# Block products for gate and value of three groups, one ScalarE silu, and a chained out-projection, in an attention and SwiGLU kernel

## The chip, the cores and the metric

The kernel runs on one core of a Trainium2 chip. A core has TensorE (PE in the views, with its weight loads as PEld), which multiplies matrices into the accumulation memory PSUM; VectorE (DVE); ScalarE (ACT); GpSimd (POOL), which does not touch PSUM here; and SyncE (SP), whose queue issues most transfers. The metric is the device time of one execution in microseconds, the median of several runs.

## What is computed

```python
# q, k, v: 4 x 8 heads x 768 x 64; heads 0, 2, 6 see all earlier keys,
# the others only the first 4 keys and a window of 64
scores = scale * q @ k.T;  scores[~mask] = -1e9
a = exp(scores - max) / sum
x = (a @ v).transpose(0, 2, 1, 3).reshape(3072, 512)
g = x @ w_gate                      # 512 x 1536
out = (g * sigmoid(g) * (x @ w_val)) @ w_out     # 1536 x 512
```

## The kernel before

The 3072 tokens are 24 tiles of 128, made in pairs from attention: load q, k and v, cast to 16 bit, transpose (on PE for the early pairs, by DMA for the later ones), scores (L570), exp on ACT (L582), a mask where needed (L590, DVE or POOL), values (L600), division by the sum (L607, L608), and a transpose that gives x with features on the partitions. Four tiles make a group, so there are groups 0 to 5; x of two groups is held at a time (`xt`).

The feed-forward part of a group has 12 tiles of 128 hidden features. A plain gate or value tile is four matmuls of 512 columns (`gate`, L762). The gate goes through tanh on ACT (L768, `g * sigmoid(g)` is `0.5 g (1 + tanh(g/2))`), then DVE multiplies twice: `stt1` (L775) makes `(1 + tanh) * g`, `stt2` (L781) multiplies by half the value and writes the hidden state `h_sb` in 16 bit. Groups 0 to 3 have plain gates and values. Groups 4 and 5 have plain gates, but their values are made of seven block products (Winograd's form of Strassen's scheme): x is cut in two halves of tokens and two of features, the weights in two halves of features and two of hidden features, and seven products of sums of blocks take the place of eight. Sums of weights (`msum`, L1058) and of x (`xsum`, L1088) are made once; `w_product` (L1108) makes one product for a pair s of hidden tiles, four matmuls of 256 columns. Products 1, 6, 7 and 4 are added one upon the other in one PSUM bank X, and after each of the first three a copy of the bank's state (r1, u2, u3) is taken, since the four result blocks need different partial sums. Product 2 goes to a bank Y, products 5 and 3 to a bank Z. The copies and adds (`w_copy`, `w_add` L1129) bring the results to SBUF, and `stt2_w` (L1152) multiplies them with the gate.

The out-projection of every group is made by seven products too (`seventh`, L866; 12 matmuls of 256 columns each), on sums of h (`hsum`, L837) and of w_out (`wsum`, L415). Before the change each product of groups 0 to 4 has a PSUM bank of its own, and DVE adds them up in the output buffer (`gathered`, L904): one copy and seven adds a group. Group 5 has a form of its own (`last_sevens`) that stores each quarter as it comes. Two halves of a group's output are stored each by one transfer.

The order is written out. Every piece of work is a task of a `Plan` with a list of engines that may run it, dependences and the buffers that it takes. `ORDER` lists all tasks, two characters a task, in one line for all engines, made by a planner outside the kernel; each engine runs its own tasks in that order. `WAYS` has a digit a task, which of its engines it takes; `SLOTS` a digit a buffer, which place of its ring. Waits follow from the dependences; every engine's queue is in order, so an instruction that waits holds up all that stand behind it on that engine.

Rings of buffers: `raw` (11 of 4 KB a partition), `hq`, `e`, `sig`, `sil` (casts, exps, tanh, first multiplies), `xb`, `xt`; and eight PSUM banks that `gv` (gate, value, block products), `o` (out-projection) and `big` (scores, attention values: two banks) share.

Of the kernel before, what the change touches and what calls it, by code (L numbers as in the profile page):

```python
# [7 lines left out]
FP = mybir.dt.float32  # L8
FH = mybir.dt.float16
# [7 lines left out]
    "06000307090A01081U1V0D041cxl1W1X0C021d1f0B20211g1e280g1i2229231h2B2A1j0m1r2C0h1Y1p1s2D1a0F1Z2N1q"  # L17
    "2X1b2E0G2O051k1l2W1t1m2F1u2L1x1v1w2f2M1n2g1y2cxk2h0n27252d241o262l2i2e2m2G0E0y2H1z2I2P0z2j2Q8m2t"
    "2R0k8w8n102o308x8o2x112p2U312J0i132V8p2K8z2y0H8q918y2k9G928r3C2n94939L2z8s3I9H323D0q9B95968t149I"
    "8u3J903L978v389C0l99983K9D9E0j2Z9M9A9J3M9F2Y9O9N0o3N9K3U339P1C3V3R2a2q2r0I3S2b9p2s16343O2u3W9k9q"  # L20
    "0r3T3P9r35363b9l2v0J3E379V3X3F1D3H3f3i3Q9Q9m3g0s1F9n9R9W3A3h9S9u0p399o9s9v3B9X2w0K9z179t3j0x3Y9w"
    "3Z0M193u9Y3a3G3l9Z3n3c3m9a1G0uA09T3v9bA13o3d0t409U3k2SA23e9c0O43A33p441A3q41459x3r2T0v42490L9y4C"
    "463y4D9f4H4A3w3x9i9g4B479d9h0P9j3s124Q4K3t4N4R9eB74O1HB24LA6BA48B8B5A7B30QB9184EAd4M0w5C1Q4ZBM15"
    "4F4PBBBP4g4G1BAsA8B40RAYAtB60N4YAxAu1KBNAvA94e5D1IBC1RBO1TAeAgAyAf1J5GATAwBD0SB0Az1EBQ5KAUBH4VAh"
    "4I1MBFBE4h5fA4BG1SAZ0T5EAa5IAi1L5FB1AbBI1OAV4J4aAnAc4bBJAC0VA5AB4fAoAA4d4l4o1NAD5gBK1P3zAG4p5nAE"
    "BL4m4S0aAH4TAjAI5JAp4WAk4U4i5L4q4jAM4v4c4n0W4rAJ5H514y4XANAK4zAF5l4k52AWAL4sAO4tAlAS4u4w0U5T54AX"
    "5m5UAq535055APAr6LAm5W565MAQ57BTBRARBU5o5NBV58BW5c594x5XBf5ABS5O5B5v5p5s5Y5w5VBh5q0YBX5t0XBY5Z5r"
    "5a0ZBd5i5b606366Be64BZ6H676w5P6I6N5QCj6K5uCUBaCk6P6EClCPBcCVBg0bCKCQCW745dCm5R7OCLCF73Cn5hBi69CN"
    "5SCMCR5x5yCOC06O615zCXC16J5e6vC2C3685kBq0f6x6572BjBrCYCGC46Q6ACIBl7P5jCHBt71Bs8e6U6RBk6VCe0eBu0c"
    "CA6WCf626SCg6B6CCJChCB6TCCBvCiCSBw6DBb70C5Bx6G6eCTByC66yBpC77F6X6Z0d7GBzC86YCZ7HC96a757CCa6n6FCb"  # L30
    "Bm6o817Q6b6c76CqCDCs826dDf7DBnCc77BoDr7E89CEE1Ds7WDt7879E2DcCdDu7XCrDdE3CtE4De7UDD7A6MCo6gDvDE7L"
    "7RDgDmDF7BCuE5DGDnCp7VDXCvDHDoDI88DYDZ6z7Y6k7bDJ7S6lDKDS7ZDa6m7j7IDb7JDTDp8f7K7cE6Dq6fDU6p7m6hE7"
    "E8E96i7dDN80EA6jDL6q86Dw7M7a7N6r6sDxDOD06t7nDy6u7p7eD1Cw7x7fDM7q8387DP8A7T8D7sCx8ED2Cz7gD3DV8B7o"
    "DhDW7h7rD47i7t7kDiEaD68NDj85D5Cy8G8YD87u8ZD7DQEc8H7vDR8I8W7y7wEtDk8J8C8X8F8T8QDl8K8L8g8UDzEb8hEu"
    "Ee8O7l8RFNE0EfEv7z848i8jD98MDC8VEg8kF0EhDAElEi8SDBEmFl8lEj8PF1EwF8Fm8aEEExFnEG8bEk8cFpEdF98dEpFq"
    "EnEBF2FrEoFAEyEqF4FBEDEzErF3FCEsECFRFsFFFSF5GcFGEFFtFDFTEHFOEJFoFPFZGYEKFUF6FaEIFEF7FVFbGjFQGZFW"
    "ENFcGdGaFuFXFJFvGeGbFYFdFKGfFxFHFeEOFLFwFyGnFfGkEMGrFIGgGsG1FzGlGhHPG2FMGiG0FhG3GtFgFiEPGoHQGuGm"
    "HLELEQGvHRGpH6GqG5FjERFkHSH7HjG6G4ESH8HkH2G7GwETHlHMG8GxEVGyH3HTGzHNH0EWHUEUEZHOHrHVGCH1HmHvH9HW"
    "HsHnGBEXHtHXHoHwHpHDGEH4HqHYHbEYHxHEGDHHH5HcHAHfHuHBHyHFHCHZG9HIHgHdHGGHGFHhHJHaHzGGHKGLGKI0HeGA"
    "GRGIGJI1HiI3I2I9GNI4GMI5GPI6IBGOGUGSIAGQI7GVGTGWINICI8GXIEIDIRIFIHISITIJIGIIILIKIOIUIMIQIXIVIPIa"  # L40
    "IWIYIZIbIc"
)
WAYS = (
    "000000000000000000000000000000000000000000000000000000000000222222202202202021110101101110110120"
    "212101100000000000000000210012022201011011000000000000002100222212001010000000000001001000000000"
    "001200002221000000001001000000001000010010000000000212210100000000010000002000000100000120010010"
    "000000000100000001200000000000000000000000000000000000000000220000001000000000100000210001001000"
    "002101120020000001001000000021000100100000000021020000000000000000010001202200200000001000000002"
    "100000000000012001020000000000000000000200000000000000001100010000000000000000000000000000000000"
    "000000000000000000000000000000000000000000000000000010000010000000000000000000000000000000000000"  # L50
    "000000000000000000000000000000000000000000000001100000000000000000000000000000000000000000000000"
    "000000000000000000000000000100011100100000000000001000000000000000000000000000000000000000000000"
    "000000000000000001001110001000000000001110110000000001000000000000010000000100000000100000000000"
    "000000000000000000000000000000000000000000011110000110000000000010111100000100001000000000000000"
    "000000000000000000000000000000000000000000000000000000000000000000000111000110000000011001011001"
    "000"
)
# [65 lines left out]
def kernel(  # L123
# [48 lines left out]
    RINGS = {"raw": 11, "hq": 5, "e": 6, "xb": 3, "xt": 2, "sig": 2, "sil": 3,  # L172
             "ps": 8, "gv": 8, "o": 8, "big": 8}
# [7 lines left out]
    for r in ("raw", "hq", "e", "xb", "xt", "sig", "sil"):  # L181
        pools[r] = ctx.enter_context(tc.tile_pool(name="p_" + r, bufs=1))
# [249 lines left out]
    def cast(n, kd, x):  # L432

        if (n, kd) not in hqs:
            hqs[n, kd] = buf("hq", [128, 1024], FH, "hq").rearrange(
                "p (k a x) -> p k a x", k=2, a=4)
# [135 lines left out]
    def exps(t, u, unit):  # L572
        e = es[t, u] = buf("e", [128, 8, 128], FH, "e")
# [63 lines left out]
    def tasks_of_pair(n):  # L637
# [21 lines left out]
        for kd in "qk":  # L659
            old = oldq if kd == "q" else older  # L660
            if n >= XPE:
# [3 lines left out]
                P.uses(cs[kd][0], "hq", *T_ev[n, kd])  # L665
# [10 lines left out]
            P.uses(cs[kd][0], "hq", tr)  # L676

    def tasks_of_tile(t):
# [13 lines left out]
        for u, unit in enumerate(units):  # L692
# [651 lines left out]
```

## Time and profile before

| | |
|---|---|
| runs | 236.73, 236.61, 236.62 us; median 236.62 |
| profiled execution | span 234.7 us from the first to the last instruction; its time as a whole is not on the page |
| instructions | 5854 |

The profile comes from one execution of the program. The span begins with the first instruction. Busy time is that of the engines' own instructions; issuing transfers is not counted. An instruction's row names the output and input tiles (`banks` is PSUM, `raw` a buffer of the raw ring) and the number of partitions by elements. "Idle before" is the time in which the engine did nothing just before the instructions of a group, with what ended it. The chain of waits goes back from the last instruction, at each step to what released it.

The first scores run at 10 us, the first feed-forward product at 19.6; the last exp runs at about 163 us, the last block product at 214, and from 218.3 on PE has only out-projection left, 120 matmuls.

### The profile page before, as it was taken

The numbers are of one execution on the slowest core, as the hardware profiler recorded it, in microseconds if no ns is written. First come the engines' busy times: TensorE is split into PE (matmuls) and PEld (weight loads), VectorE is DVE, ScalarE is ACT, GpSimd is POOL, SyncE is SP. The second block draws the span as 40 slices with busy tenths as digits, with TensorE's granted clock in tenths as the row PEclk, the third lists the DMA queues.
The fourth block names the chain that finished last, engine by engine and source line by source line (L and its number), as shares of the span: only waits on it lengthen the run. The fifth ranks groups of instructions, "written<-read, shape, count | busy, mean of one in ns | idle before, by whom it ended". The sixth has DMA issues, their size and how long they took to land.

```text
span 234.7 us, 5854 instructions
## 1 busy us (share of the span) xinstructions
PE 228.7 (97%) x2283; PEld 152.8 (65%) x2283; DVE 204.4 (87%) x369; ACT 157.9 (67%) x256; POOL 136.4 (58%) x150
## 2 busy tenths in 40 slices
PE   7899999999999999999999999999999999999994
PEld 2577865654457778645564556776876767668883
DVE  1889989989989998989879974889979999999954
ACT  3599999679899779856786389768554643553110
POOL 7485499864695300469840887273096930593950
PEclk9999999999999999999999999999999999999999
DMA  6999999999999998998994621500920000220054
GB/s 180 351 343 366 327 340 369 343 341 314 271 259 220 236 251 166 270 179 178 234 217 124 102 45 31 62 3 2 225 45 3 3 0 3 89 89 4 0 201 159
DMA packets 67196, 40.76 MB, mean 174 GB/s; under 512 B 25184, under 2 KB 61024, under 8 KB 67168
## 3 DMA queue, kind: packets, MB, share of 16 engines
q1 hardware_dynamic: 65104, 37.37, 64.5%
q10 hardware_dynamic: 2064, 3.02, 3.6%
q8 instruction: 18, 0.29, 0.5%
q14 instruction: 10, 0.08, 0.1%
HBM read 28.31 MB, written 6.29 MB: 147 GB/s over the span
## 4 chain that ended last, share of the span: by engine, by line
PE 89%; ACT 3%; DMA 2%; DVE 2%; SPq 2%; issue 1%; POOL 0%; ACTq 0%; POOLq 0%
PE banks L762 45%; PE banks L866 23%; PE banks L1108 8%; PE banks L570 6%; PE banks L600 6%; DMA raw<-in_k_dram 2%; ACT e L582 2%; SPq L352 1%; PE banks L476 1%; PE banks L624 1%; DVE xb L608 1%; ACT kT L209 0%; SPq L357 0%; DVE kT L211 0%; DVE sil L775 0%
## 5 line engine op out<-in xcount | busy, mean ns | idle before, releaser
L762 PE MATMUL banks<-xt,wg_sb 128*128 128x512 f16 (+1 forms) x304 | 71.6, 368 | 0.1
L582 ACT ACTIVATE e<-banks 128x1024 f16<-128x1024 f32 (+2 forms) x68 | 59.4, 911 | 11.0 <-PE banks L570 6.3
L768 ACT ACTIVATE sig<-banks 128x512 f32<-128x512 f32 (+1 forms) x76 | 42.8, 577 | 30.6 <-PE banks L762 23.2
L762 PE MATMUL banks<-xt,wv_sb 128*128 128x512 f16 (+1 forms) x208 | 48.2, 363 | 0.0
L762 PEld LDWEIGHTS <-wg_sb 128*128 128x128 f16 x304 | 28.6, 98 | 25.9 <-issue 0.5
L866 PEld LDWEIGHTS <-h_sb 128*128 128x128 f16 x420 | 40.2, 98 | 7.4
L775 DVE SCALAR_TENSOR_TENSOR sil<-sig,banks 128x512 f32<-128x512 f32 (+1 forms) x52 | 32.8, 641 | 5.8 <-ACT sig L768 4.7
L781 DVE SCALAR_TENSOR_TENSOR h_sb<-sil,banks 128x512 f16<-128x512 f32 (+1 forms) x52 | 32.8, 640 | 3.1 <-PE banks L762 2.7
L837 POOL TENSOR_TENSOR h_sb<-h_sb 128x768 f16<-128x768 f16 x13 | 21.3, 1644 | 21.1 <-DVE hs_sb L837 17.2
L762 PEld LDWEIGHTS <-wv_sb 128*128 128x128 f16 x208 | 19.1, 98 | 17.2
L590 POOL TENSOR_TENSOR e<-e,m 128x640 f16<-128x640 f16 (+1 forms) x16 | 26.6, 1670 | 5.7 <-ACT e L582 4.7
L904 DVE TENSOR_TENSOR out_sb<-banks,out_sb 128x512 f32<-128x512 f32 x37 | 25.0, 684 | 2.1 <-PE banks L866 1.7
L866 PE MATMUL banks<-wt_sb,h_sb 128*128 128x256 f16 x216 | 26.0, 273 | 0.1
L866 PE MATMUL banks<-wo_sb,h_sb 128*128 128x256 f16 x204 | 24.9, 273 | 0.0
L209 ACT COPY raw<-banks 128x512 f32<-128x512 f32 x26 | 14.6, 588 | 15.2 <-DVE h_sb L1152 5.5
L570 PEld LDWEIGHTS <-kT 64*128 64x128 f16 x472 | 14.5, 94 | 9.2 <-issue 8.7
L570 PE MATMUL banks<-qT,kT 64*128 64x128 f16 x472 | 19.9, 218 | 0.1
L211 POOL CAST hq<-raw 128x1024 f16<-128x1024 f32 (+1 forms) x9 | 8.0, 893 | 20.1 <-DMA raw<-in_k_dram 18.2
L600 PEld LDWEIGHTS <-e 128*128 128x128 f16 x472 | 17.3, 97 | 3.6 <-POOL e L590 0.3
L600 PE MATMUL banks<-vt,e 128*128 128x65 f16 x472 | 18.6, 193 | 0.0
L608 DVE TENSOR_TENSOR xb<-banks,rc 128x512 f16<-128x512 f32 x24 | 16.6, 691 | 0.8
L775 DVE SCALAR_TENSOR_TENSOR banks<-sig,banks 128x512 f32<-128x512 f32 x24 | 16.3, 687 | 0.2 <-ACT sig L768 0.2
(85 smaller groups left out, 318.6 us busy)
## 6 DMA issues: line engine op xcount, KB each, us to landing
raw<-in_v_dram SPq DMA_DIRECT2D x12, 512.0 KB, 6.8
raw<-in_q_dram SPq DMA_DIRECT2D x8, 512.0 KB, 5.6
raw<-in_k_dram SPq DMA_DIRECT2D x8, 512.0 KB, 5.0
raw<-in_moe_w_gate_dram SPq DMA_DIRECT2D x6, 512.0 KB, 8.2
raw<-in_moe_w_val_dram SPq DMA_DIRECT2D x6, 512.0 KB, 8.3
raw<-in_moe_w_out_dram SPq DMA_DIRECT2D x6, 512.0 KB, 8.4
out_dram<-out_sb SPq DMA_DIRECT2D x6, 512.0 KB, 3.5
raw<-in_q_dram SPq DMA_DIRECT2D x8, 256.0 KB, 6.6
```

The costliest lines, as they stand in the source:

```text
L570: nc.tensor.matmul(sc[:, c:c + n, :], weights, moving, start=first, stop=last)
L582: nc.scalar.activation(out=to, in_=src, func=AF.Exp, scale=scale)
L590: ENG[task().way].tensor_tensor(out=ev, in0=ev, in1=mm, op=ALU.mult)
L600: nc.tensor.matmul(avs[t][:, odd, n * 66:n * 66 + 65], ee, vv, start=(m == 0), stop=(m == len(bl) - 1))
L608: nc.vector.tensor_tensor(out=xb.rearrange("p n o d -> p o n d"), in0=av[:, :, :, 0:64], in1=rc.to_broadcast([128, 2, 4, 64]), op=ALU.mult)
L762: nc.tensor.matmul(ps, wsb[:, kk, j * 128:(j + 1) * 128], xt[:, kk, c[0]:c[1]], start=(kk == 0), stop=(kk == 3))
L768: nc.scalar.activation(out=sg[g, j, c], in_=gs[g, j, c], func=AF.Tanh, scale=0.5)
L775: nc.vector.scalar_tensor_tensor(out=sl[g, j, c], in0=sg.pop((g, j, c)), scalar=1.0, op0=ALU.add, in1=gs.pop((g, j, c)), op1=ALU.mult)
L781: nc.vector.scalar_tensor_tensor(out=hs[g, j][:, c[0]:c[1]], in0=sl.pop((g, j, c)), scalar=0.5, op0=ALU.mult, in1=vs.pop((g, j, c)), op1=A ...
L837: ENG[T_hs[g, x][part].way].tensor_tensor(out=to, in0=a, in1=b, op=op)
L866: nc.tensor.matmul(rooms[g, p][:, x, lo:hi], left[:, j, 128 * x:128 * x + 128], right[:, j, lo:hi], start=(on is None and (j == 0 if apart ...
L904: nc.vector.tensor_tensor(out=cell(*to), in0=room, in1=plus, op=ALU.add)
```

## The change

- Groups 3, 4 and 5 (`FULL`) have both gate and value made of block products; before, only the values of groups 4 and 5 were. The gate's weight sums lie in the rooms of kT[0] and vt[0] once batch 2 no longer needs them.
- For each pair s of hidden tiles, quarter by quarter (c11, c21, c22, c12: half of tokens by half of hidden features), ACT makes silu in one operation (`AF.Silu`), and DVE one multiply by the value, of which c21 is read straight from bank X and the others from PSUM after an add in place. Groups 0 to 2 keep tanh and two multiplies.
- c11 is one DVE add of bank Y and r1 (before: a copy of Y and an add on POOL or DVE).
- Out-projection of groups 0 to 4: products 1, 6, 7, 4 are chained in one bank, with copies r1, u2, u3 and c21 on ACT or DVE; product 3 is added onto product 5; three DVE adds a group in place of seven. Its sums wait for quarters of h.
- The rings hq, e, sig and sil become one ring `t2` of 16 buffers of 2 KB.
- ORDER, WAYS and SLOTS are new for the whole kernel.

```diff
-    RINGS = {"raw": 11, "hq": 5, "e": 6, "xb": 3, "xt": 2, "sig": 2, "sil": 3,
-             "ps": 8, "gv": 8, "o": 8, "big": 8}
+    RINGS = {"raw": 11, "t2": 16, "xb": 3, "xt": 2, "gv": 8, "o": 8, "big": 8}
...
-    ONTO = {2: 1, 3: 5}
+    ONTO = {True: {2: 1, 3: 5}, False: {6: 1, 7: 1, 4: 1, 3: 5}}
...
-        on = ONTO.get(p) if g == NG - 1 else None
+        on = ONTO[g == NG - 1].get(p)
...
+    def o_copy(g, name):
+        room = rooms[g, {"r1": 1, "u2": 6, "u3": 7, "c21": 4}[name]]
+        if name == "c21":
+            to = cell(1, 0)
+        else:
+            to = o_cells[g, name] = buf("t2", [128, 2, HM], FP, "oc")
+        copy(T_ga[g, name], to, room)
+
+    def o_add(g, name):
+        p, to, other = {"c11": (2, (0, 0), "r1"), "c22": (5, (1, 1), "u3"),
+                        "c12": (3, (0, 1), "u2")}[name]
+        nc.vector.tensor_tensor(out=cell(*to), in0=rooms[g, p], in1=o_cells.pop((g, other)),
+                                op=ALU.add)
...
+        p1 = product(1, quarter[0, 0] + wo, ["o"])
+        r1 = copied("r1", [p1])
...
+        p6 = product(6, T_hs[g, 2] + T_ws[2] + [r1])
+        u2 = copied("u2", [p6])
+        p7 = product(7, T_hs[g, 3] + T_ws[3] + [u2])
+        u3 = copied("u3", [p7])
+        p4 = product(4, quarter[1, 1] + T_ws[4] + [u3])
+        c21 = copied("c21", [p4] + free[1])
...
-    WINO = {"v": (4, 5), "g": ()}
+    FULL = (3, 4, 5)
...
+    SPENT = [kT[0].rearrange("p a b c d -> p (a b c d)"), vt[0].rearrange("p a b c -> p (a b c)")]
...
     def w_add(mat, g, s, name):
-        to = w_cell(mat, g, s, name)
-        other = w_cell(mat, g, s, "y2") if name == "c11" else w_rooms[mat, g, s, "Z"]
-        ENG[T_wc[mat, g, s, name].way].tensor_tensor(out=to, in0=other, in1=to, op=ALU.add)
...
+        on, other = {"c11": ("Y", "r1"), "c22": ("Z", "u3"), "c12": ("Z", "u2")}[name]
+        room, other = w_rooms[mat, g, s, on], w_cells.pop((mat, g, s, other))
+        to = w_cells[mat, g, s, name] = (
+            other if mat == "g" else
+            buf("gv", [128, 2, 256], FP, "gv") if name == "c22" else room)
+        nc.vector.tensor_tensor(out=to, in0=room, in1=other, op=ALU.add)
+
+    def silu(g, s, name):
+        src = w_rooms["g", g, s, "X"] if name == "c21" else w_cells["g", g, s, name]
+        nc.scalar.activation(out=w_cells["g", g, s, name], in_=src, func=AF.Silu)
+
+    def mul(g, s, name):
+        x, y = {"c11": (0, 0), "c21": (1, 0), "c12": (0, 1), "c22": (1, 1)}[name]
+        j = NK * y + 2 * s
+        val = w_rooms["v", g, s, "X"] if name == "c21" else w_cells.pop(("v", g, s, name))
+        nc.vector.tensor_tensor(
+            out=h_sb[:, g % 2, j:j + 2, 256 * x:256 * x + 256], in0=val,
+            in1=w_cells.pop(("g", g, s, name)), op=ALU.mult)
```

What the strings say, counted task by task from ORDER and WAYS (before, after):

| tasks | before | after |
|---|---|---|
| PE: gate tiles / value tiles (of 512 columns; the eight halves of group 0 count as four) | 72 / 48 | 36 / 36 |
| PE: block products of gate and value | 42 | 126 |
| PE: out-projection products | 42 | 42 |
| ACT: tanh of groups 3 to 5 / silu | 36 / 0 | 0 / 36 |
| ACT: copies of block products / of the out-projection | 25 / 6 | 46 / 18 |
| DVE: multiplies of groups 3 to 5 | 72 | 36 |
| DVE: adds / copies of block products | 13 / 5 | 54 / 8 |
| DVE: adds and copies of the out-projection | 43 | 26 |
| POOL: adds of block products / weight sums of gate and value | 5 / 3 | 0 / 9 |
| whole casts of q and k on ACT / DVE / POOL | 10 / 4 / 6 | 6 / 1 / 13 |
| output halves stored from SP / from ACT | 6 / 4 | 8 / 2 |

In the new ORDER PE works from group 2's first out-projection product on as follows (`out2.p1` is product 1 of group 2, `sc20.1` the second set of scores of tile 20, `val` attention values, `wp3.1.6g` product 6 of group 3's gate, pair 1):

```
out2.p1 sc20.0 sc20.1 val19.1 val19.0 out2.p2 sc21.0 sc21.1 sc20.2 out2.p6 val17.1 sc21.2 val17.0
out2.p7 sc22.1 sc22.2 sc22.0 out2.p5 val20.1 val20.0 out2.p4 sc23.3 sc23.2 val21.1 val21.0 out2.p3
wp3.1.1g sc23.1 sc22.3 sc23.0 wp3.2.1g wp3.0.1g wp3.2.2g wp3.1.6g wp3.1.2g wp3.1.2v wp3.0.6g val22.1
val22.0 wp3.1.5g wp3.1.7g wp3.0.7g wp3.0.5g wp3.1.1v wp3.2.6g
```

and ACT around its last exp:

```
ex23.2 oc2.c21 ex22.3 ex23.1 wy3.0.r1g ex23.0 wy3.1.u2g wy3.0.u2g silu3.2.c11 wy3.0.u3g wy3.1.r1v
wy3.2.u2g wy3.0.r1v silu3.1.c21 silu3.1.c11 wy3.2.u3g wy3.1.u2v silu3.0.c21
```

All 68 exps and 40 tanh of the new order stand before its first silu. In the old order the gates and values of group 3 stand among the scores of tiles 16 to 23; in the new one group 3 begins with `wp3.1.1g`, and the last scores (tile 23) stand there too.

More of the change, by code (lines that the diff above doesn't have):

```diff
@@ L22 @@
[L22 to L26, printed above, removed]
@@ L896, in gathered @@
             nc.vector.tensor_tensor(out=c, in0=room[:, x, lo:hi], in1=c, op=ALU.add)
-        elif g == NG - 1 and name == "c11":
+        elif name == "c11":
             x, lo, hi = PARTS[part]
             copy(T_ga[g, name, part], cell(*to)[:, x, lo:hi], room[:, x, lo:hi])
-        elif other is None:
-            copy(T_ga[g, name], cell(*to), room)
         else:
-            plus = ends["r1"] if g == NG - 1 and name == "r6" else cell(*other)
+            plus = ends["r1"] if name == "r6" else cell(*other)
             nc.vector.tensor_tensor(out=cell(*to), in0=room, in1=plus, op=ALU.add)
@@ L1001, in tasks_of_sevens @@
         if g == NG - 1:
-            last_sevens(g, lower, upper, wo, free, old, T_h, product, sums, gather, finish)
+            last_sevens(g, quarter, wo, free, of_part, product, sums, gather, finish)
             return
-        p1 = product(1, lower + wo, ["o"])
-        r1 = gather("r1", [p1] + free[1])
-        sums(1, lambda part: [y for j in range(3 * part, 3 * part + 3)
-                              for y in T_h[j] + T_h[j + NK]] + old)
-        sums(3, lambda part: [T_hs[g, 1][part]])
@@ L1069 @@
                     (lambda mat=mat, i=i, kk=kk: msum(mat, i, kk)),
-                    deps=[y for n in range(6) for y in T_w[mat, n]] + before,
-                    takes=(["hq"] if i == 4 else ["e"]) if mat != EARLY
-                    else [] if kk else ["raw"],
+                    deps=[y for n in range(6) for y in T_w[mat, n]] + before + spent,
+                    takes=["raw"] if mat == "v" and kk == 0 else [],
                     after=T_mw[mat, i][:1]))
@@ new lines @@
+                a = P.add(f"gate{g}.{j}.{c[0]}", ["PE"],
+                          (lambda g=g, j=j, c=c: gate(g, j, c, wg_sb, gs)),
+                          deps=xs[c[0] // 128:c[1] // 128] + [T_w["g", j // 2][j % 2]],
+                          takes=["gv"])
+                th = P.add(f"tanh{g}.{j}.{c[0]}", ["ACT"],
+                           (lambda g=g, j=j, c=c: tanh(g, j, c)), deps=[a], takes=["t2"])
+                s1 = P.add(f"stt1 {g}.{j}.{c[0]}", ["DVE"],
+                           (lambda g=g, j=j, c=c: stt1(g, j, c)), deps=[th], takes=["t2"])
@@ L1253 @@
+                P.uses(a, "gv", s1)
+                P.uses(T_first_x[g], "xt", a)
                 was = [T_p[g - 2, p] for p in ((6, 7) if j < NK else (3, 4))] if g > 1 else []
                 was += T_hs[g - 2, 4] if g > 1 and j < NK else []
-                if g not in WINO["g"]:
-                    P.uses(th, "sig", s1)
-                if g in WINO["v"]:
-                    cells = [T_wc["v", g, j % NK // 2, y] for y in below]
-                    s2 = P.add(f"stt2 {g}.{j}.{c[0]}", ["DVE"],
-                               (lambda g=g, j=j: stt2_w(g, j)), deps=[s1] + cells + was)
-                    T_h.setdefault(j, []).append(s2)
-                    P.uses(*((th, "gv") if g in WINO["g"] else (a, "gv")), s2)
-                    P.uses(T_wc["v", g, j % NK // 2, head], "raw", s2)
-                    continue
+                P.uses(th, "t2", s1)
```

396 lines of the change are left out of this document (168 added, 228 removed).

## The prediction, made before the changed kernel was run

> **What bounds the kernel now.** First the page: the span, the busy shares, the granted clock, and the chain of waits.
>
> ```profile
> span 234.7 us, 5854 instructions
> PE 228.7 (97%) x2283; PEld 152.8 (65%) x2283; DVE 204.4 (87%) x369; ACT 157.9 (67%) x256; POOL 136.4 (58%) x150
> PEclk9999999999999999999999999999999999999999
> PE 89%; ACT 3%; DMA 2%; DVE 2%; SPq 2%; issue 1%; POOL 0%; ACTq 0%; POOLq 0%
> ```
>
> TensorE (PE) is busy 97% of 234.7 us at full clock and carries 89% of the chain that ended last. VectorE (DVE) follows with 87%. Second the view by windows: each row gives the busy microseconds of PE, weight loads, DVE, ScalarE (ACT) and GpSimd (POOL), then clock, DMA share and GB/s. I cut at the stages of the work.
>
> ```profile
> 19.60:67.20 47.60, 47.59 (x486) 29.07 (x486) 44.59 (x88) 42.76 (x69) 34.34 (x39) 1.00 1.13 330
> 67.20:106.50 39.30, 39.29 (x450) 27.14 (x448) 36.08 (x64) 31.81 (x52) 15.39 (x17) 1.00 1.11 222
> 106.50:131.30 24.80, 24.80 (x220) 13.73 (x220) 21.80 (x37) 16.62 (x27) 14.18 (x12) 1.00 0.82 178
> 131.30:158.70 27.40, 27.31 (x311) 17.84 (x309) 20.80 (x37) 20.67 (x32) 19.02 (x22) 1.00 0.32 45
> 158.70:171.00 12.30, 12.30 (x149) 9.14 (x149) 12.02 (x25) 8.16 (x14) 2.87 (x3) 1.00 0.52 119
> 171.00:218.30 47.30, 47.30 (x350) 33.98 (x348) 45.55 (x75) 23.48 (x43) 28.97 (x22) 1.00 0.08 27
> 218.30:234.70 16.40, 13.10 (x120) 11.49 (x118) 10.57 (x19) 1.56 (x3) 7.80 (x5) 0.98 0.36 129
> ```
>
> The reader is to see that from 19.6 to 218.3 us PE is idle for 0.11 us in all, although DVE is at 94% (44.59 of 47.60) in the first stretch and at 96% (45.55 of 47.30) in the last. So end time is PE work, and work of other engines is paid only where it makes PE wait. Third the chain in order of time (start, us, what), for the price of a product:
>
> ```profile
> 57.75 9.50 PE banks L762 x44
> 159.15 0.54 PE banks L1108 x4
> 186.57 1.75 PE banks L1108 x16
> 218.30 13.11 PE banks L866 x120
> 231.43 0.42 DVE out_sb L896
> ```
>
> A 512-column matmul costs 9.50/44 = 0.216 us, a 256-column one 1.75/16 = 0.1094 (13.11/120 gives the same in the out-projection). A gate or value tile is four of the first, 0.864; a block product four of the second, 0.4375.
>
> **TensorE's share of the change.** Gone: 36 gate tiles of groups 3 to 5 and 12 value tiles of group 3, 48 x 0.864 = 41.5 us. Added: 3 groups x 3 pairs of tiles x 2 matrices x 7 = 126 block products where 42 stood, so 84 x 0.4375 = 36.8 us. The balance is **-4.7 us**. The out-projection keeps its 12 matmuls a product. Since PE is never idle before, there is no old wait to win back. Below that I allow 1.4 us more, from fewer changes between short attention matmuls and wide ones (the change row above: 0.54 where 0.4375 is due, so 0.1 a change; 40 changes after the start against 44 give 0.4) and from a start that may shift by 1 us, since some early evacuations change engine.
>
> **The other engines.** Rows of groups (count | busy us, mean ns | idle before), and two of the timeline for the spacing of instructions back to back:
>
> ```profile
> L768 ACT ACTIVATE sig<-banks 128x512 f32<-128x512 f32 x68 | 40.0, 599 | 30.6 <-PE banks L762 23.2 <-DVE banks L775 2.9 <-DVE xb L608 2.8
> L209 ACT COPY raw<-banks 128x512 f32<-128x512 f32 x26 | 14.6, 588 | 15.2 <-DVE h_sb L1152 5.5 <-DVE out_sb L904 4.6 <-PE banks L1108 3.8
> L209 ACT CAST hq<-raw 128x1024 f16<-128x1024 f32 x10 | 10.4, 1043 | 0.1
> L211 POOL CAST hq<-raw 128x1024 f16<-128x1024 f32 x6 | 6.2, 1035 | 18.2 <-DMA raw<-in_k_dram 17.6 <-DVE m L289 0.3 <-POOL vt L211 0.2
> L1152 DVE SCALAR_TENSOR_TENSOR h_sb<-banks,raw 128x512 f16<-128x512 f32 x24 | 15.9, 682 | 0.2
> L1129 POOL TENSOR_TENSOR raw<-raw 128x512 f32<-128x512 f32 x5 | 6.8, 1365 | 12.3 <-ACT raw L209 12.3
> L1058 POOL TENSOR_TENSOR raw<-wv_sb 128x768 f16<-128x768 f16 x3 | 4.9, 1644 | 0.1
> L582 ACT ACTIVATE e<-banks 128x1024 f16<-128x1024 f32 x44 | 44.0, 1025 | 5.0 <-PE banks L570 2.4 <-PE banks L600 1.0 <-issue 0.9
> 196.19 1.89 DVE L1152 SCALAR_TENSOR_TENSOR h_sb<-banks,raw 128x512 f16<-128x512 f32 x3
> 173.10 1.56 ACT L209 COPY raw<-banks 128x512 f32<-128x512 f32 x3 [0.77 <-DVE raw L1129]
> ```
>
> Full-size DVE instructions come every (1.89 - 0.68)/2 = 0.60 us, ACT copies every (1.56 - 0.59)/2 = 0.49. From the strings (counts in the section on the change): DVE loses 72 gate and value multiplies, 13 cell adds, 5 copies and 43 gathers of the out-projection, and gets 36 products, 54 adds, 8 copies and 26 gathers: 133 become 124, -9 x 0.60 = -5.4 us. ACT changes 36 tanh for 36 silu (I take the tanh's 0.60 us; a silu that reads SBUF is not in the trace, and the nearest cast from SBUF, 64x512, took 0.615) and gets 33 more copies, 33 x 0.49 = 16 us; it gives four whole q/k casts away (-4.2). So ACT goes from 158 to about 171, 74% of 232. POOL takes seven of those casts (+7.2) and six weight sums (+9.8) and loses five adds (-6.8), among smaller moves: about 140 of 232. No engine but PE is full on average. These terms I cost at nothing: PE's 232 us cover them. If that cover goes, it goes in one of two places, which are the rivals below. The four extra sums of x for group 3 and the eight of the gate weights lie on POOL and DVE ahead of their products; the weight sums go to rooms of batch 2's keys and values, which the order frees some 13 us of PE work before product 7 first reads them.
>
> Stores: eight halves of the output are issued on SP instead of six. A store waits in SP's queue for its cells, and behind it wait loads and transposes. The one of group 0 stands ahead of the loads of q9, k10, k11, x11 and q10; its cells are due with PE's own order there, so nothing is late. DMA's share is 0.82 and 0.32 in the windows from 106.5 to 158.7, so the last pair's transposes, which move about 18 us of PE work forward, find room.
>
> **The one new instruction outside the sums: a table load.**
>
> ```profile
> L209 ACT ACT_TABLE_LOAD x1 | 1.3, 1283 | 0.7 <-PEq L1325 0.7
> ```
>
> Exp, Tanh and Copy ran through the whole execution on one load of 1.28 us. In the new order every exp and tanh stands ahead of the first silu, and silus alternate with copies only. If silu needs another table, that is one more load. ACT is in order, so the copies behind it are up to 1.28 us late; the tightest chained products shortly behind it have 1.3 to 2.2 us of other PE work as cover, of which a copy takes 0.59. So the price lies between 0 and 1.28, and I take **0.6**. The Trainium skill's page "ScalarE: Activation LUTs" (section "Table sets: the hidden batching unit") speaks against such a change: functions are to be grouped by set. Its section "What ACT_TABLE_LOAD costs" puts a switch at about 2.66 us with the drain. By that price, wholly exposed, the result would be 2.1 us later than mine; the 1283 ns of the load agree with this row, the drain is not a row here.
>
> The sum: 236.62 - 4.7 + 0.6 = **232.5 us**. The profiled execution shows a span of 234.7; the median of the runs is 1.9 above it, taken as what lies around the span, so I subtract from the median.
>
> **Rivals.**
>
> *A, the attention loses its filler.* From group 2's first out-projection product to the last exp, PE's old order holds 15 gate and value tiles of group 3 (13 us) among the scores. None is left: by the rows' prices PE has 17.6 us of work there (30.2 before), DVE 18.2, ACT 16.6. DVE is over PE for that stretch, and the loop of a tile shows its latency: scores, exp, mask, values.
>
> ```profile
> 160.55 0.55 PE banks L570 x16
> 161.11 0.90 PE banks L600 x25
> L590 DVE TENSOR_TENSOR e<-e,m 128x1024 f16<-128x1024 f16 x14 | 9.9, 714 | 0.0
> ```
>
> One loop is 0.55 + 1.03 + 0.71 + 0.45 (half the value matmuls) = 2.7 us; exposed once, the time is **235.2**. For it: the overloaded stretch. Against: from 19.6 to 67.2 DVE was at 94% and ACT at 90%, with the same loops, and PE did not wait.
>
> *B, slower: chained products wait in a lockstep of in-order queues.* A product may add to a bank only when the copy (or add) of its last state is done. There are 92 such links against 24. PE work between two ends of a link, counted in the order: under 1.1 us at 2 links in both orders, under 1.5 at 12 (3 before), under 2 at 23 (4 before). A bare link needs 0.59 and is covered everywhere. But 27 of the silus wait for a DVE add, and a copy queued behind such a silu needs 0.59 + 0.60 + 0.68 = 1.87 where DVE is one instruction late. At the 12 links with about 1.3 us that is 0.56 each, 6.7 us: 236.62 - 4.7 + 6.7 = **238.6**, slower. It decides from 8 such waits (4.7/0.56). For it: thrice the short links, a wait stops all of PE's queue, in which out-projection and block products of every chain stand behind. Against: 24 links before, two of them under 1.1 us, cost no idle time, and DVE's load is lower after.
>
> *C, it doesn't do what it says: silu and copy need different tables.* They alternate 41 times; 42 loads x 1.28 give 54 us, some **286**. Against: Copy and Exp shared a table in all of this trace.
>
> *D, narrow products cost more than half a wide one.* Break-even is 192 matmuls of 0.216 against 336: 0.1234 us each. At the 0.54 of the chain's row for four (0.135) the added work is 8.6 us dearer, **241**. Against: 16 in a row and 120 in a row ran at 0.109. The Trainium skill ("TensorE: Matmul & The Clock Gate", section "Back-to-back issue gap") gives a sustained spacing of 131 ns at 512 columns and 81 at 128, which would put a 256-column one near 98 (an estimate from that page) and make the change a loss of 7.8 us; this trace, with 216 ns at 512, contradicts it.
>
> **How the numbers follow.** Forecast, PE stays full and its work shrinks (231 to 234): 0.60. A 0.17, B 0.18, C 0.04, D 0.01. About 0.2% can be told from no change, 0.47 us. Faster: 0.60 + 0.14 of A = 0.74; same: 0.02 of A and 0.02 of B = 0.04; slower: 0.01 of A, 0.16 of B, C and D = 0.22. The range, 230.5 to 238.6, takes in the forecast (its low end is 236.62 - 4.7 - 1.4), A, and half of B: about 0.85.
>
> **What would show it.** Right: PE idle near zero between 20 and 218 us, a block product at 0.4375, 120 out-projection matmuls at the end in 13.1, one new table load near the last exp, ACT busy 170 to 175, DVE 195 to 200. A: PE idle ahead of value or score matmuls shortly before the load, released by DVE or ACT. B: PE idle ahead of block products, released by ACT copies. C: dozens of loads. D: 256-column products at 0.12 or more with weight loads back to back. Wrong altogether if the early stretch moves, which I leave as it is.

## The result, and the profile after

The changed kernel took **251.19 us** (median of 4 runs, 250.47 to 251.88) against 236.68 for the kernel before on the same chip: a ratio of 1.0611 [1.0589, 1.0632], so 14.5 us slower. The forecast was 232.5 with a range up to 238.6: wrong in sign and out of its range, by 18.7 us.

The page of the changed kernel: span, busy shares, PE's busy tenths in 40 slices, its granted clock, and the chain of waits by engine.

```profile
span 248.7 us, 6208 instructions
PE 229.4 (92%) x2427; PEld 169.1 (68%) x2427; DVE 216.6 (87%) x367; ACT 171.8 (69%) x284; POOL 149.7 (60%) x156
PE   7899999999977899799999697989999999999994
PEclk9999999999999999999999889799999999999998
PE 66%; DVE 23%; issue 6%; DMA 2%; SPq 1%; POOL 1%; ACT 0%; DVEq 0%; ACTq 0%; POOLq 0%
```

PE's share of the chain fell from 89% to 66%; VectorE has 23% of it in place of 2%. ACT's 171.8 us are the forecast's 171. VectorE's 216.6 are not its 195 to 200, although the instructions are those counted. The windows (us busy of PE, weight loads, DVE, ACT, POOL; clock, DMA share, GB/s) say where PE stands idle (0.11 us in all before, from 19.6 to 218.3):

```profile
20.00:80.00 60.00, 56.55 (x562) 34.24 (x563) 55.00 (x97) 47.97 (x79) 44.85 (x50) 1.00 1.10 303
80.00:140.00 60.00, 54.94 (x634) 36.78 (x634) 53.84 (x88) 47.41 (x75) 36.99 (x33) 1.00 0.92 181
140.00:160.00 20.00, 16.66 (x220) 13.31 (x220) 17.71 (x30) 11.21 (x18) 11.01 (x10) 0.83 0.29 62
160.00:220.00 60.00, 58.79 (x574) 52.13 (x572) 54.85 (x88) 42.46 (x79) 33.44 (x25) 1.00 0.13 40
```

PE's idle time is 3.45 + 5.06 + 3.34 + 1.21 = 13.1 us, most of it between 20 and 160, where the old and new work are much alike and the forecast expected nothing; the stretch of block products from 160 on is nearly full. From 140 to 160 the clock was 0.83 on average, another 20 x 0.17 = 3.4 us.

What the lost time is made of shows in VectorE's groups by shape (count | busy us, mean ns). The kernel before, then the changed one:

```profile
L837 DVE TENSOR_TENSOR h_sb<-h_sb 128x768 f16<-128x768 f16 x9 | 4.9, 549 | 0.0
```

```profile
L802 DVE TENSOR_TENSOR h_sb<-h_sb 128x768 f16<-128x768 f16 x9 | 7.4, 822 | 0.5 <-POOL hs_sb L802 0.4
...
L802 DVE TENSOR_TENSOR hs_sb<-h_sb 128x768 f16<-128x768 f16 x4 | 5.1, 1282 | 0.0
...
L1042 DVE TENSOR_TENSOR kT<-wg_sb,kT 128x768 f16<-128x768 f16 x2 | 2.5, 1269 | 0.0
```

The same operation on the same shape took 549 ns before and up to 1282 on average after. VectorE has 68 16-bit sums and masks there. Against the means of their shapes in the kernel before, 22 of them are longer by over 60 ns, and all 68 together take **18.1 us** more (the extra time, below). In the kernel before one of 56 is longer, by 0.4 us. By the trace all 22 begin while GpSimd runs an instruction, and of the 43 that begin while GpSimd stands still none is longer; before the change 55 of the 56 begin so. The timeline of the changed kernel shows one of the 22 (start, us, engine, line, what; in brackets the idle time before and what ended it):

```profile
137.62 1.83 POOL L802 TENSOR_TENSOR h_sb<-hs_sb,h_sb 128x768 f16<-128x768 f16 x1
137.98 1.88 DVE L802 TENSOR_TENSOR h_sb<-h_sb 128x768 f16<-128x768 f16 x1
...
139.97 0.63 DVE L802 TENSOR_TENSOR h_sb<-hs_sb,h_sb 128x768 f16<-128x768 f16 x1
...
140.75 0.69 DVE L608 TENSOR_TENSOR xb<-banks,rc 128x512 f16<-128x512 f32 x1
...
141.49 0.77 PE L570 MATMUL banks<-qT,kT 64*128 64x128 f16 x12 [2.43 <-DVE xb L608]
```

VectorE's sum starts at 137.98, inside a sum of GpSimd that ends at 137.62 + 1.83 = 139.45, and ends at 139.86: 0.41 us after it, where it needs 0.55 alone. That is how an instruction looks that stands still while GpSimd runs. Behind it in VectorE's queue stands the division `xb`, which frees the bank for the next scores, and PE waits 2.43 us for it.

My theory from this, **T1**: the new ORDER and WAYS let such instructions meet, VectorE stands still, and its delay reaches PE through short waits. The rivals: **T2**, transfers come late in the new order; B of the prediction, the chained products; and the clock as a cause of its own.

### The profile page after: what moved, and what is told of

Its sections match the earlier page's. It is cut to its first block, busy times and chain, and to the rows that moved or that the text cites. A ratio compares the mean times of both kernels' runs of the same rounds, so it can differ in the third digit from the quotient of the medians.

```text
span 248.7 us, 6208 instructions
## 1 busy us (share of the span) xinstructions
PE 229.4 (92%) x2427; PEld 169.1 (68%) x2427; DVE 216.6 (87%) x367; ACT 171.8 (69%) x284; POOL 149.7 (60%) x156
## 4 chain that ended last, share of the span: by engine, by line
PE 66%; DVE 23%; issue 6%; DMA 2%; SPq 1%; POOL 1%; ACT 0%; DVEq 0%; ACTq 0%; POOLq 0%
PE banks L1092 18%; PE banks L762 18%; PE banks L831 17%; PE banks L570 6%; DVE e L590 5%; PE banks L600 4%; DVE h_sb L778 3%; DVE h_sb L802 2%; DVE sil L772 2%; DMA raw<-in_q_dram 2%; DVE xb L608 2%; PE banks L476 1%; DVE h_sb L1125 1%; DVE vt L215 1%; DVE banks L1115 1%
## 5 line engine op out<-in xcount | busy, mean ns | idle before, releaser
L582 ACT ACTIVATE e<-banks 128x1024 f16<-128x1024 f32 (+2 forms) x68 | 58.4, 913 | 18.5 <-PE banks L570 16.3
L762 PE MATMUL banks<-xt,wg_sb 128*128 128x512 f16 (+1 forms) x160 | 35.5, 358 | 2.3 <-DVE e L590 1.4
L762 PE MATMUL banks<-xt,wv_sb 128*128 128x512 f16 (+1 forms) x160 | 35.7, 358 | 1.0 <-DVE sil L772 0.4
L802 POOL TENSOR_TENSOR hs_sb<-h_sb 128x768 f16<-128x768 f16 x8 | 13.1, 1642 | 32.1 <-DVE h_sb L1125 26.4
L209 ACT COPY wc<-banks 128x512 f32<-128x512 f32 x39 | 22.0, 593 | 9.5 <-PE banks L1092 9.4
L772 DVE SCALAR_TENSOR_TENSOR sil<-sig,banks 128x512 f32<-128x512 f32 (+1 forms) x40 | 24.5, 627 | 2.9 <-ACT sig L768 2.7
L778 DVE SCALAR_TENSOR_TENSOR h_sb<-sil,banks 128x512 f16<-128x512 f32 (+1 forms) x40 | 24.7, 628 | 1.9 <-PE banks L762 1.2
L768 ACT ACTIVATE sig<-banks 128x512 f32<-128x512 f32 (+1 forms) x40 | 21.4, 556 | 6.2 <-PE banks L762 2.6
L762 PEld LDWEIGHTS <-wg_sb 128*128 128x128 f16 x160 | 14.6, 98 | 16.2 <-issue 2.9
L590 DVE TENSOR_TENSOR e<-e,m 128x1024 f16<-128x1024 f16 (+1 forms) x25 | 21.2, 866 | 0.1
L1115 DVE TENSOR_TENSOR banks<-banks,wc 128x512 f32<-128x512 f32 x27 | 18.5, 692 | 0.7 <-PE banks L1092 0.5
```

The source lines that it names most:

```text
L209: nc.scalar.copy(out=dst, in_=src)
L582: nc.scalar.activation(out=to, in_=src, func=AF.Exp, scale=scale)
L590: ENG[task().way].tensor_tensor(out=ev, in0=ev, in1=mm, op=ALU.mult)
L762: nc.tensor.matmul(ps, wsb[:, kk, j * 128:(j + 1) * 128], xt[:, kk, c[0]:c[1]], start=(kk == 0), stop=(kk == 3))
L768: nc.scalar.activation(out=sg[g, j, c], in_=gs[g, j, c], func=AF.Tanh, scale=0.5)
L772: nc.vector.scalar_tensor_tensor(out=sl[g, j, c], in0=sg.pop((g, j, c)), scalar=1.0, op0=ALU.add, in1=gs.pop((g, j, c)), op1=ALU.mult)
```

## The experiments

### Making the sums meet, or not, by their engine alone

In the changed kernel two instructions that met go to VectorE and six that met to GpSimd; in the kernel before three go each way, so that sums meet there. Two of the lines of WAYS (0 and 1 are a task's engines):

```diff
-    "200000000000021020010200000000010000000010000001000000001011100100001111000000000000000000000000"
+    "200000000000021020010200000000000000000010001001000000001011111100000111000000000000000000000000"
```

> The changed kernel with eight 16-bit sums and masks given to the other engine of VectorE and GpSimd (two to VectorE, six to GpSimd), nothing moved in the order; the work of both engines, at the durations without an overlap, changes by under 3 us on VectorE and +8 us on GpSimd. Theory T1 (a 16-bit two-input VectorE instruction on SBUF data that starts while a GpSimd instruction runs stands still until that one ends): the eight are picked so that fewer pairs meet; the extra time of these VectorE instructions falls from some 18 us to 10-13 us and the kernel from 251.2 to about 243 us (241 to 245.5). Rival A (attention lost the work that filled it): four masks become 1.6-2.2 us on GpSimd instead of 0.5-0.7 us on VectorE inside the loop scores, exp, mask, values, so 251 to 254 us. Rival B (lockstep of the chained products): none of their links is touched, 251 us within 1.

```diff
-    "000000000000000000000000000100011100100000000000001000000000000000000000000000000000000000000000"
+    "000000000000000000000000000100011100000000000000001000000000000000000000000000000000000000000000"
```

> The kernel before, with nothing of the change, only six 16-bit sums and masks given to the other engine (three to VectorE, three to GpSimd; the work of both engines without an overlap changes by under 1.5 us). T1: the six are picked so that more pairs meet; the extra time of 16-bit VectorE instructions goes from under 1 us to 10-15 us and the kernel from 236.7 to about 247 us (243 to 250), with PE idle in the stretches where the pairs meet. Rivals A and B live in parts that only the change has: 236 to 238 us.

Measured: after_flip8 251.36 us, 1.0625 [1.06, 1.0651], no gain: the pairs that I separated met others instead, 18 instructions stood still and the extra time stayed at 18.1 us. It says nothing for or against T1. before_flip6 took 242.49, 1.0243 [1.0226, 1.026]: six digits cost 5.84 us. Its meetings were 8, 6.6 us of extra time; I had expected more of both, and the time came under its range of 243 to 250 us, but loss and extra time go together. The groups by shape of this kernel:

```profile
L837 DVE TENSOR_TENSOR hs_sb<-h_sb 128x768 f16<-128x768 f16 x6 | 5.8, 972 | 0.0
...
L1058 DVE TENSOR_TENSOR raw<-wv_sb,raw 128x768 f16<-128x768 f16 x4 | 3.6, 910 | 0.0
```

Shapes that took 549 and 547 ns in the kernel before took 972 and 910 here, in the same order. The three that moved to GpSimd also take longer there by themselves (1.64 us for 0.55 at 128x768), but no wait of VectorE there names GpSimd, and all waits of PE from 20 to 220 us, 4.8 us, name VectorE. So it is the meetings that make this kernel, whose PE was full, 2.4% slower.

### The meeting by itself

A kernel of its own: eight VectorE instructions of one kind, alone or beside GpSimd sums of 128x768 in 16 bit.

```diff
+    PHASES = [(sum16, None), (stt16, None), (copy16, None), (cast16, None), (scale16, None),
+              (max16, None), (sum32, None), (bank32, None),
+              (sum16, p_sum), (stt16, p_sum), (copy16, p_sum), (cast16, p_sum),
+              (scale16, p_sum), (max16, p_sum), (sum32, p_sum), (bank32, p_sum),
...
```

> Not the reference's computation: constants only, the output is zeros. 21 stretches, each with eight VectorE instructions of one form on 128x768 elements (bank form: 128x512), the first eight stretches alone, the others beside five GpSimd instructions of one form. T1 (a 16-bit two-input VectorE instruction on SBUF data that starts while a GpSimd instruction runs stands still until that one ends): the 16-bit sum takes 0.55 us alone; beside GpSimd's 16-bit sums (1.64 us each) the ones that start inside a GpSimd instruction end 0.35 to 0.45 us after its end, the longest at 1.5 us or more; forms with a PSUM operand, with f32 data, the reduce used as a cast and the scalar_tensor_tensor form keep their time alone within 5%. Rival (both engines share the memory's bandwidth): every form grows by about the same factor, 1.2 to 2, and none stands still.

Its kinds ran in another order than written, so each meeting is read from the timeline. Three of them, and then two groups by shape, over all their instances, alone or met:

```profile
18.18 2.30 POOL L66 TENSOR_TENSOR z<-x,y 128x768 f16<-128x768 f16 x1
...
18.91 1.98 DVE L42 TENSOR_TENSOR c<-a,b 128x768 f16<-128x768 f16 x1
...
22.61 2.30 POOL L66 TENSOR_TENSOR z<-x,y 128x768 f16<-128x768 f16 x1
...
23.34 2.38 DVE L45 SCALAR_TENSOR_TENSOR c<-a,b 128x768 f16<-128x768 f16 x1
...
44.11 2.24 POOL L66 TENSOR_TENSOR z<-x,y 128x768 f16<-128x768 f16 x1
...
44.77 0.68 DVE L63 TENSOR_TENSOR r<-bank,f 128x512 f32<-128x512 f32 x1
```

```profile
L57 DVE TENSOR_REDUCE c<-f 128x768 f16<-128x768 f32 x16 | 15.2, 951 | 0.5
...
L63 DVE TENSOR_TENSOR r<-bank,f 128x512 f32<-128x512 f32 x24 | 16.3, 680 | 0.0
```

A 16-bit sum that takes 546 to 559 ns alone took 1.98 us inside a GpSimd sum, and ended 0.41 after it. The multiply-add of two SBUF operands (0.96 alone) took 2.38 and waits too, and so do the 32-bit sum (0.95 alone, 2.40 met), copies and casts: there my expectation, which had only the 16-bit sums wait, missed. Two kinds don't wait: one that reads a PSUM bank, 0.68 every time, and the reduction, 951 on average. The reduction met only GpSimd's casts here; beside a two-input instruction of GpSimd the kernel before shows it: one of 64x512 that begins at 78.08 inside a mask (78.06 to 79.46) takes 0.68 us, its time alone. It goes both ways: GpSimd's sum took 1.63 us alone and 2.30, as in two of these rows, where it started inside a VectorE instruction of the waiting kind.

The Trainium skill states this rule ("SBUF — State Buffer", section "Who interferes with whom"): VectorE and GpSimd share a pair of SBUF ports, a VectorE instruction with two SBUF inputs and a GpSimd instruction that reads SBUF exclude each other, whichever starts first keeps the pair for its whole instruction, and a reduction never takes part. The 1.98 against 0.56 us, the 0.68 and the 951 ns agree with it. The prediction didn't draw on it.

### Orders planned anew

All of ORDER and WAYS anew, nothing else, so that fewer sums meet; the changed kernel and, as a control of how well I plan, the kernel before.

```diff
-    "06000307090A01081U1V0D041cyH0C1d1W1X021f0B1g20211e0g281i2223291h2A0m2B1j1r0h2C1Y1p2D1s0F1a1Z2N1q"
...
```

> The changed kernel, every instruction of PE and SP in its old place, with VectorE, ScalarE and GpSimd work put in another order and partly on another of these engines so that few 16-bit VectorE instructions start during a GpSimd one on the path. All 92 chained links and the attention without its filler remain. T1: extra time of 16-bit VectorE instructions on the path nearly gone, about 227 us (224.5 to 231). Rival A: at least 235 us, rival B: at least 238 us, since both hold whatever the engine assignment of the sums.

> The kernel before with its VectorE, ScalarE and GpSimd work put in another order by the same procedure, PE and SP as they were. About 233 us (231 to 236) by every theory. What it tells is the difference to after_replanned, the worth of the changed products when both orders are found alike: T1 expects after_replanned to be 4 to 7 us faster than this one, A and B expect it 0 to 6 us slower.

after_replanned took 246.64 us (1.042 [1.0385, 1.0455]), far from the expected 227, with the extra time down from 18.1 to 5.1 us. before_replanned took 245.18 (1.0359 [1.0341, 1.0377]): with 7.3 us of extra time and no other edit, my orders lose 8.5 us on the old kernel too, so a planned order of mine is no clean test of the change. But the first shows the second fault. The chain of waits of after_replanned at its longest gap of PE (start, us, what), and the windows there:

```profile
91.27 4.40 DMA qT<-hq
...
96.06 0.82 ACT e L582
96.89 0.04 issue
96.93 1.70 PE banks L600 x28
```

```profile
91.70:96.90 5.20, 0.00 (x0) 0.00 (x0) 0.21 (x1) 4.95 (x9) 0.00 (x0) 0.72 0.96 236
96.90:101.00 4.10, 4.07 (x42) 3.12 (x41) 2.19 (x4) 2.31 (x4) 2.08 (x3) 0.52 0.94 285
```

PE, VectorE and GpSimd all stand still for 5.2 us: value matmuls wait for an exp, and that for a transpose by DMA (whose source `hq` and the exp's `e` share the ring `t2`). Then the clock is half for 4 us. That is T2's mark, so I cut the loads, which run on the same queue.

### Half the loads

From pair 5 on, q, k and v are loaded with four of the eight heads, which the casts read twice.

```diff
+            hh = H if n < 5 else H // 2
...
-                in_={"q": q, "k": k, "x": v}[kind][b, :, sl, :].rearrange(
+                in_={"q": q, "k": k, "x": v}[kind][b, 0:hh, sl, :].rearrange(
```

> The changed kernel; the 21 loads of q, k and v for pairs 5 to 11 bring four heads instead of eight (256 KB instead of 512 KB) and the casts read these four twice, so the output differs. T1: the extra time of 16-bit VectorE instructions stays at 15 to 18 us and the time at 249 to 252 us. Theory T2 (the DMA queue: loads and transposing DMAs of the later pairs land late and the attention that waits for them leaves PE idle): PE's gaps between 85 and 130 us go, 243 to 247 us. Rivals A and B: 251 within 1.

> The same edit of the loads in the kernel before. T1: 236 within 1 us. T2, if the queue is late in both kernels: 2 to 4 us faster; if only the changed kernel meets it: within 0.7 us.

after_thinload took 249.93 us (1.0562 [1.0529, 1.0595]), only 1.3 less than the change, with the extra time unchanged at 18.5; before_thinload 236.70 (1.0005 [0.9995, 1.0014]). Loads are not what the change loses first. With the new order and half loads it is another matter:

> after_replanned (246.6 us, 2.4 us of standing still) with the half loads of after_thinload (four heads of q, k and v for pairs 5 to 11, output differs). Theory T1 alone (standing still is all of the loss): no reason for a gain, 246 to 247.5 us. Theory T1+T2 (two faults of the order lie one behind the other: VectorE standing still, and behind it loads and transposing DMAs that land late; in the changed kernel the first hides the second, so that half loads alone gave 1.3 us): here the second is bare, about 240.5 us (238.5 to 243), and PE's gap of 5.2 us at 92 us goes. A and B: 246 to 247.5.

237.52 us (1.0036 [1.002, 1.0051]): 9.1 less than the same order with whole loads. (The 2.4 us of extra time in its expectation is a miscount of mine; it was 5.1, and 5.9 here.) So once most of the sums keep apart, loads are what is late.

Orders that also counted the loads and transposes, by prices from these runs:

> The changed kernel with the DMA queue's order changed too: VectorE, ScalarE, GpSimd and SP in another order and assignment in which VectorE's 16-bit instructions don't stand still on the path and each load lands before its cast's turn; PE's order as it was, all products, links and silus as they were. T1+T2: PE idle in 20 to 220 us from 19 us to 7-10 us, 234 us (231 to 238). T1 alone as in after_replanned: 244 to 248. A: not under 235, B: not under 238.

> As after_replan2, with PE's own order open too (the same products, other places). T1+T2: 231.5 us (228 to 236), 2 to 3 us under after_replan2. A and B as there.

> The changed kernel with all its data, products, links and silus, and another order of all five engines, made so that neither fault is left: VectorE's 16-bit instructions don't stand still on the path, and the DMA queue isn't asked to change between plain and transposing DMAs where both are waited for. T1+T2: 235 us (231.5 to 240), PE idle in 20 to 220 us under 9 us, granted clock 0.99 or more. T1 alone: as after_replanned, 245 to 248. A: not under 235, B: not under 238.

> As after_replan3_32, another such order. T1+T2: 235 us (231.5 to 240). T1 alone, A and B as there.

All four missed: 247.03 (1.0445 [1.0408, 1.0482], extra time 14.0 us), 245.5 (1.0382 [1.0361, 1.0403], 13.5), 243.23 (1.0295 [1.0251, 1.0339], 4.3; part of its output comes from other values, which part I did not trace) and 243.49 (1.0284 [1.0266, 1.0302], 8.8). They missed in two ways. In the first, which keeps PE's order, the instructions of VectorE and GpSimd meet again, and PE is idle for 11.8 us from 20 to 220. In the other three PE is idle there for 7.0, 3.7 and 2.5 us, as expected, but its own work grew: it is busy for 230.2, 229.8 and 231.2 us, against 225.1 in after_replanned_thin, which keeps the change's PE order. Counted in the traces, PE goes from one kind of matmul to another (scores, attention values, wide tiles, block products, out-projection, transposes) 187 to 193 times in these three and 149 times in the change's order. At the 0.1 us that the prediction took for such a change, some 40 more would be 4 us (an estimate; no run changes this count alone).

### Each fault cut short in the change's own order

So I left ORDER and WAYS of the change as they are and made GpSimd's masks and most of its sums four columns wide: the same instructions with the same waits, done soon. (Two fills with zeros at the start come in addition.)

```diff
+    def thin(task, *aps):
+        if task.way != "POOL":
+            return aps
+        return [x[(slice(None),) * (len(x.shape) - 1) + (slice(0, 4),)] for x in aps]
...
+        ev, mm = thin(task(), ev, mm)
...
+            to, a, b = thin(T_hs[g, x][part], to, a, b)
```

> The changed kernel in its own order and assignment; of GpSimd's 16-bit sums and masks, 45 of 58 treat 4 columns of the last axis instead of all (what they leave out is left unsummed, so the output differs); VectorE's are whole, and each still waits for its inputs as before. T1 (VectorE's 16-bit instructions stand still while a GpSimd instruction runs): with GpSimd's sums over in some 0.1 us the extra time falls from 17 us to under 4.5 us and the time from 251.2 to about 244.5 us (242 to 247). T1+T2 says the same, since the late loads behind it take back the rest. A and B: 250.5 to 252.

> after_thinsum with the half loads of after_thinload as well (alone they gave 1.3 us). T1+T2: both faults gone in the changed kernel's own order, 239 us (236 to 241.5), so the two together give more than the sum of each. T1 alone: as after_thinsum less 1.3 us, 243. A and B: 249 to 251.

> The kernel before with the same cut of GpSimd's 16-bit sums and masks. T1: hardly a VectorE instruction stands still there (0.6 us), so no gain: 236.6 us within 0.7. Rival (GpSimd's sums are simply too slow and come late): a gain here too, 1.5 us or more.

| the change's order | whole loads | half loads |
|---|---|---|
| GpSimd's sums whole | 251.2 | 249.9 |
| GpSimd's sums cut short | 243.5 | 238.4 |

All three times came as expected: after_thinsum 243.53 (1.029 [1.0256, 1.0324]), after_thinsum_thinload 238.38 (1.0071 [1.0054, 1.0087]), before_thinsum 236.25 (0.9983 [0.9974, 0.9993]). Cutting the sums is worth 7.7 us in the change and 0.4 in the kernel before; halving the loads 1.3 before that cut and 5.1 after it; both 12.8. VectorE's extra time falls to 5.5 us (under 4.5 was expected). Cutting the sums also takes GpSimd's own time away (84.4 us busy instead of 149.7), so this pair alone doesn't tell a meeting from a late result; before_flip6, where GpSimd's load stays (139.2 us against 136.4), and the waits of PE in the change from 20 to 220 us, which but for one of 0.3 us name VectorE, speak for the meeting. Of after_thinsum, its chain by engine, two waits between 80 and 120 us, and a step of the chain (start, us):

```profile
PE 60%; DVE 16%; DMA 15%; issue 3%; ACT 2%; POOL 1%; SPq 1%; DVEq 0%; ACTq 0%; POOLq 0%
```

```profile
POOL vt L216 <- DMA raw<-in_v_dram: 8.1, 1, 8.1
...
DVE vt L220 <- DMA raw<-in_v_dram: 2.0, 1, 2.0
```

```profile
88.50 7.54 DMA raw<-in_v_dram
```

DMA has 15% of the chain, where it had 2% in the change: a load of values is on it for 7.54 us, and a reduction on VectorE, with masks and cells queued behind it, waits for it. Counted in ORDER it is the load of pair 7's values, the eighth of its kind before and the eleventh after. Its issue on SP, in the kernel before and in the changed one:

```profile
67.79 0.52 SPq L357 DMA_DIRECT2D raw<-in_v_dram  x1
```

```profile
89.05 0.84 SPq L357 DMA_DIRECT2D raw<-in_v_dram  x1
```

With both cut, PE's windows and busy times are these:

```profile
20.00:80.00 60.00, 57.79 (x581) 35.64 (x582) 53.94 (x100) 48.53 (x81) 35.57 (x52) 1.00 0.98 267
80.00:140.00 60.00, 58.38 (x714) 39.97 (x709) 53.41 (x99) 50.45 (x80) 16.43 (x33) 1.00 0.65 136
140.00:160.00 20.00, 18.66 (x246) 16.20 (x241) 17.72 (x31) 16.24 (x26) 11.01 (x16) 1.00 0.15 41
160.00:220.00 60.00, 59.88 (x567) 53.34 (x566) 55.60 (x91) 38.93 (x74) 7.61 (x20) 1.00 0.13 37
```

```profile
PE 225.7 (95%) x2427; PEld 167.5 (71%) x2427; DVE 207.9 (88%) x369; ACT 171.2 (72%) x284; POOL 84.3 (36%) x156
```

Idle are 2.21 + 1.62 + 1.34 + 0.12 = 5.3 us in place of 13.1, the clock is full, and PE's work is 228.7 - 225.7 = 3.0 us less than in the kernel before.

### Two last orders

> The changed kernel, complete, PE's order as it was, with VectorE, ScalarE, GpSimd and SP re-ordered so that under 4 us of VectorE's 16-bit work stands still and the later pairs' loads are issued before they are missed. T1+T2: 236 us (232 to 241), PE idle in 20 to 220 us under 10 us. A: not under 235, B: not under 238.

> As after_replan4_43, another such order: 236 us (232 to 241) by T1+T2.

240.66 us (1.0171 [1.0133, 1.0208]), at the upper end of its range, with 3.4 us of extra time, and 247.39 (1.0438 [1.0421, 1.0456]; part of the output from other values, untraced here too), a miss, with 10.5 us of extra time where under 4 was planned. The first is the fastest whole form of the change that I found, 10.5 us under the change as made and still 4 over the kernel before. Its longest waits of PE between 20 and 160 us:

```profile
PE banks L762 <- DMA xt<-xb: 2.1, 1, 2.1
PE banks L570 <- DMA qT<-hq: 1.5, 1, 1.5
```

Both are transposes by DMA: T2 again. Whether an order exists with which the change is faster than 236.6 stays open.

## Why the forecast was wrong

**The step that failed** is the one on the other engines: "These terms I cost at nothing: PE's 232 us cover them." It took from ORDER and WAYS only how many instructions each engine gets, and priced each at its duration before. On this chip the duration of a VectorE sum depends on what GpSimd does at that moment, and that is what the strings decide. The 9 instructions fewer should have brought VectorE to 195 to 200; 18.1 us of standing still brought it to 216.6. The sentence "Wrong altogether if the early stretch moves, which I leave as it is" named one place (PE is idle for 3.45 us from 20 to 80): the first meeting comes at 23.07 us, since a mask went to GpSimd just ahead of another that stayed on VectorE. In the kernel before both ran on VectorE. The changed kernel's timeline:

```profile
22.61 2.13 POOL L590 TENSOR_TENSOR e<-e,m 128x1024 f16<-128x1024 f16 x1
...
23.07 2.03 DVE L590 TENSOR_TENSOR e<-e,m 128x640 f16<-128x640 f16 x1
```

**Transfers**: I looked at the stores and at the last pair's transposes, and said that nothing is late. The loads of the pairs in the middle were not compared, and they are the second fault, worth 1.3 us in the change as it stands and 5.1 once the first is gone.

**The size.** Against the forecast the change lost 18.7 us: 13.1 of idle PE, 3.4 of half clock, and PE's term. That term, -4.7, was 1.7 too large by the busy time of the run with both cuts (-3.0). These make 18.2; the 0.6 that the forecast had for the table load is part of the idle time. They divide PE's time in the profiled execution and are not what each alone would be worth: after_thinload, profiled without a half clock, was 1.3 us faster and not 3.4. Two pieces of the changed kernel's chain:

```profile
164.09 20.10 PE banks L1092 x184
...
233.61 11.80 PE banks L831 x108
```

A block product ran as priced (20.10/184 = 0.1092 a matmul), and so did the end (11.80/108 gives the same). Where the 1.7 us are shows when each matmul is counted up to the start of the next, in the kernel before and in the run with both cuts: the wide tiles went by 41.9 us (41.5 forecast), the added block products took 37.4 (36.8), and the same score and value matmuls took 33.9 in place of 32.7, where the forecast expected no more. GpSimd's listed terms add up to 136.4 + 7.2 + 9.8 - 6.8 = 146.6 and not to the forecast's 140; it took 149.7.

**The table load** came once, as forecast. Its row among the groups, and the window from its begin on, of PE alone:

```profile
L1119 ACT ACT_TABLE_LOAD x1 | 1.3, 1283 | 0.0
```

```profile
163.00:220.00 57.00, 56.49 (x552) 1.00 0.13 38
```

PE was idle for 57.00 - 56.49 = 0.51 us in all in these 57 us, so the load cost at most that; I had taken 0.6.

**The rivals.** C and D did not come: one load, and 0.109 a matmul. B did not come: 58.79 of 60 us busy among the chained products, 59.88 with the faults cut, and no wait of PE from 20 to 220 us names an ACT copy. A is the half-open one: two gaps of 2.43 and 1.85 us stand ahead of score and value matmuls, released by VectorE, in the place that it named. VectorE's delay there comes from meetings (in the rows above), and with both cuts 1.34 us are left. But it reaches PE because no gate or value tiles stand there any more; how much of a delay the old filler would have hidden, no run tells.

**Open**: the 5.3 us of idle time in the run with both cuts, of which its 5.7 us of extra VectorE time (GpSimd's casts were left whole) may be a part, are not traced one by one; 4.3 us of PE's waits there name VectorE, the longest 1.3, and 0.8 GpSimd.

## What to carry to other kernels

Where an order written out decides which engine does what and when, the sum of durations by engine is not enough: lay VectorE's instructions with SBUF operands beside GpSimd's and price each meeting at what is left of the other's instruction. This kernel's PE was full with VectorE at 87% in an order in which one of VectorE's 56 such instructions met GpSimd; six of them on the other engine cost 5.84 us. A new order has to avoid the meetings again. To test that without planning a new one, cut the suspected partner's instructions to a few columns and leave order and waits as they are, and do so for two suspects together, since the second fault hides behind the first.

## What the runs showed of the hardware

VectorE's sums, multiply-adds, copies and casts of SBUF data waited for a running GpSimd sum to its end (a sum of 0.55 us took 1.98), and GpSimd's sums for theirs (1.63 us became 2.30); an instruction with a PSUM operand (0.68) or a reduction (0.68 for 64x512) did not. A cast on GpSimd is enough: 2.7 us of the change's extra time belong to instructions that begin inside one. That was the surprise of the case, with 18.1 us of it.

Short gaps of PE can cost twice. After the gaps of 2.43 us (at 139.06) and 1.85 us (at 152.44) the granted clock (in these windows the column before the last two) fell to half for some 3 us in the change, while PE was busy:

```profile
142.00:144.00 2.00, 2.00 (x20) 1.43 (x15) 2.00 (x4) 1.41 (x2) 0.63 (x1) 0.50 0.34 52
...
155.00:159.00 4.00, 4.00 (x39) 2.81 (x35) 2.20 (x5) 0.05 (x1) 3.83 (x5) 0.57 0.01 2
```

The Trainium skill ("TensorE: Matmul & The Clock Gate", section "Part 1: The HAM clock gate (the "warmup" mystery)") puts that at an idle window of about 3.4 us; here 1.85 were enough. Size alone does not decide it: after_thinload has gaps of 2.43 us (at 139.55) and 2.02 us (at 152.52), and its clock is 1.00 in every window from 20 to 220.
